# A new hand-written order, with limits on transfers in flight, for a chunked RWKV-7 attention and MLP kernel

## The chip, the cores and the metric

The kernel runs on one core of a Trainium2 chip. Its engines each run their own list of instructions: TensorE (PE, with its weight loads counted apart as PEld), VectorE (DVE), ScalarE (ACT), GpSimd (POOL) and SyncE (SP), which here does nothing but issue DMA transfers. The engines wait for one another by semaphores. The metric is device time in microseconds (us), the median over several executions.

## The reference

The inputs r, k, v, w, a and b have 4 batches, 8 heads, 768 tokens and 40 channels, all in float32. For each batch and head a 40x40 state is carried along the tokens; then x, of 3072 tokens by 320 channels, goes through a two-layer MLP with a quick GELU.

```python
for t in range(S):
    y[:, :, t] = einsum('bhd,bhde->bhe', r_t, state)
    Sa = einsum('bhde,bhe->bhd', state, a_t)
    state = state * w_t[:, :, None, :] - einsum('bhd,bhe->bhde', Sa, b_t) \
          + einsum('bhd,bhe->bhde', v_t, k_t)
x = y.transpose(0, 2, 1, 3).reshape(3072, 320)
h = x @ w_in                                 # 320 -> 2048
out = (h / (1 + exp(-1.702 * h))) @ w_out    # 2048 -> 320
```

## The kernel before, in words

The 768 tokens are cut into 12 chunks of 64, and the 4 batches into 2 pairs: 24 units of one chunk and one pair. Within a unit the recurrence is solved as a triangular system of 64x64 for each head, so that nearly all work is small matmuls, four of them side by side in quarters of the array. A unit i goes through five steps; the line numbers are those of the profile:

- `decay` (from line 552) sums the logarithms of w on PE (`ps_cum`, `ps_cumc`) and takes their exponentials on ACT (`FT`, `GT`, `wch`, `G`).
- `prep` (from 627) scales the loaded operands by them: `ak` by `FT` at line 633 and by `GT` at 638, `b` at 635, `kh` and `bh` at 641, on DVE or POOL. PE forms the scores: `score_A` into `ps_A`, `score_RV` into `ps_RV`, and in the next step `score_N` into `ps_N`.
- `inverse` (from 676) inverts the triangular matrix by five `level`s. Each has matmuls into `ps_level`, copies to `W` (765) and `E` (767), a transpose `ES` (716) and a spreading `EX` (721 on ACT, 723 on DVE or POOL). `off_one` and `off_two` (`Tc` copies at 811, `ps_Q`, `ps_T`) join the blocks into `T` (844).
- `solve` (from 850) turns the state (`ps_zT`), reads it (`ps_rz`, copied to `zr` at 883), builds `B` (905, 908), multiplies by `T` (`ps_X`, `M` at 921), and forms the output and the new state in one group `ps_y`. The output is copied (956) and scaled (966, `x`), written to DRAM (`part_with`) and read back turned (`get_back`, into `xT`).
- After the second unit of a chunk comes `mlp(c)` (from 991): eight groups q of `ps_up` matmuls, each followed by one GELU on ACT (1004) into one of four `g` tiles, then for each pair the `ps_down` matmuls, a copy and an add into the one `ob` tile (1031, 1033), and a store. In the last group the 320 columns are done in two halves.

Tiles have few slots: two each for `ak`, `b` and `rv`, three for `xT`, one for `x` and `ob`. The PSUM is used as four pairs of banks; which pair a result gets is part of the order.

All this is recorded as 2709 tasks. `Plan.listed` (line 89) then reads the string `ORDER` (line 109): one word for each task, with its number, a letter for its engine (p PE, d DVE, a ACT, g POOL, s SP) and a digit. The tasks are issued in exactly this order, so each engine runs its own in this order; an engine that waits holds back everything listed for it later. For p, d, a and g the digit is the PSUM pair. For s, the transfers, it is `t.window`, a limit which `transfer` (line 331) turns into a wait:

```python
begun.append(queue.dma_start(dst, src).ins)
if t.window and len(begun) > t.window:
    tc.add_manual_dep(begun[-1], begun[-1 - t.window].name, ...)  # few transfers under way
```

A word `330s4` means: task 330 is issued on SP, and it waits until the transfer that was begun four before it has landed. No digit means no limit. One task can begin two transfers. All transfers go through SP's queue, except one half of the last store, which ACT issues.

Of the kernel before, what the change touches and what calls it, by code (L numbers as in the profile page):

```python
# [124 lines left out]
56d 480s 479s3 78s4 481g 482d 57d 327d3 380d0 81s4 570a 236p1 59g 392a2 389p0 237p1 328d3 393d2 329g 330s4 390a0 484g 238p1  # L125
73a 486p3 487d3 240p0 491p3 74d 239a1 381p2 472s4 492d3 473s 493d3 241p0 494a3 382d2 242p0 485d 529d 394p2 79s 488p1 75d 76d
339a 489d1 530p3 532a3 496d 243p0 251p1 395d2 531a3 497a 82a 77g 340d 252p1 557s3 558s4 548p3 83d 85d 396p2 495d 549a 244p0
84d 245p0 550a3 338s4 397d2 86g 253p1 398d2 533p2 551g 399g 534a2 554a 254p1 498p2 500d2 560s4 501d 562d 568p3 499a2 331s 609d
246p0 247p0 556s4 559s4 535p2 255p1 561d 474a 248a0 569d3 249d0 400s 401s2 571p3 536d2 610p0 256p1 572d3 475d 564d 563d 257p1
612a0 574a3 258p1 573d3 576d 575d 577d 537p2 402p3 502g 403p3 404p3 611a0 250s 578p0 538a2 539d2 259a1 702s 566p2 405p3 580d0  # L130
581d 260d1 567d2 565g 406p3 407p3 579a0 503p1 408p3 504a1 582g 409p3 553s 505d1 410p3 694p2 424p1 425p1 426p1 613p0 427p1 703s
695a 706s 428p1 429p1 411p3 506d 696a2 583p2 555d 430p1 585d2 614d0 431p1 432p1 412a3 433p1 584a2 586d 446p3 507d 708d 508p0
699s 698s4 447p3 587d 552s 510d0 511d 434a1 413p2 512a 588p1 414p2 509d0 415p2 513p0 707d 590d1 591d 416p2 589a1 592d 417p2
785s3 593p1 700a 515d0 514d0 418p2 516d 709g 419p2 517d 420p2 421p2 518p0 595d1 594d1 519d0 523d0 422p2 782s2 524d0 520d 435p1
436p1 437p1 697d 438p1 423a2 521a0 525p2 704s2 439p1 526d2 440p1 522a0 441p1 716p0 596d 718d0 527p2 442p1 443p1 444p1 597g
528d2 445a1 719d0 540p2 448p3 598p1 717d0 720g 721d 261s2 722a 617p0 618a0 541d2 599d1 602d1 542p2 619d0 615p0 711g 601a1 600d
544d2 449p3 603a1 604a1 781s 723p1 616d0 605p0 450p3 606a0 607p0 451p3 452p3 710d 701d 545g 608d0 546s 783s 705s 927s 725d1
724d1 726d 543d2 620p0 727a 773p1 930s 778s 547s 453p3 621d0 774a 754d 728p2 622p0 454d3 455d3 729d2 456s 457p3 775a1 776g
730d2 784s 786g 779a 777s 624d0 458p3 623d0 625g 731d 793p1 833d 732a 459p3 733p2 789g 460p3 626s 734a2 794d1 735d2 714p0 790g
736d 461p3 780d 737g 1009s 918p1 755p2 923s 462p3 715d0 756a2 627s 757a2 788d 463p3 738p0 787d 464p3 739a0 740d0 919a 795p2  # L140
465d3 758p0 1006s 466d3 798a2 921d 650p3 467s 759d0 920a1 651p3 924a 928s 796d2 712p1 797d2 652p3 922s 800d 799g 653p3 932d
801a 654p3 834p0 655p3 713d1 656p3 657p3 835d0 760p2 836d0 925d 658p3 761a2 659p3 762p1 660a3 741d 628p0 742d 926s 629p0 630p0
763d1 802p2 764d1 631p0 803a2 804d2 632p0 805d 633p0 806a 743p3 634p0 746d3 635p0 747d3 837p1 931g 748d3 636p0 838a1 1007s
749d3 637p0 807p2 744d3 933g 638a0 639p1 808d2 640p1 791p3 745a 809d2 672p0 810d 792d3 811a 750p2 641p1 751a2 812p3 642p1
813a3 814d3 752p2 643p1 753d2 644p1 815d 645p1 816a 765p3 839p2 766d3 646p1 840a2 647p1 817p3 648p1 818a3 819d3 767p2 820d
649a1 821d 673p0 769d2 929s 768d2 770g 822p3 934d 674p0 825a3 826a3 940p1 827a3 675p0 1151s 828a3 935d 943a1 771s 661p2 823d3
662p2 941d1 1154s 824a 663p2 942d1 997p3 945d 944g 664p2 998a 1002s 978d 938p1 946g 665p2 939d1 666p2 772s 667p2 668p2 829p1
669p2 999a3 1000d 1001s 830d1 670p2 1003a 1011d 676p0 671a2 1004d 831p3 841p1 677p0 832d3 1005s 842d1 936p3 843d1 678p0 937d3
844p2 679p0 845d2 947p1 1010g 680d0 846p3 948a1 681d0 1012d 682s 683p2 847d3 1013g 1008s 848d3 1019p0 1014g 949d1 684p2 1022a0
1230s 849d 1233s 979p3 685p2 980a3 950d 850s 1020d0 981a3 951g 1142p1 1021d0 686p2 1024d 1143a 1147s 1023d 1025g 982p3 1057d  # L150
687p2 1152s 952p0 851s 983a3 1145g 688p2 1156d 1146s 953a0 954d0 984p3 1144a1 955d 1148a 689p2 956d 985a3 1149d 986p0 690p2
987a0 1150s 988d0 957p1 691a2 863p3 958a1 692d2 864p3 959d1 865p3 693s 960d 866p3 961d 1026p0 867p3 1027a0 1028d0 868p3 1029d
1155g 869p3 1157d 1030a 1058p2 870p3 871p3 1059a2 872p3 1060d2 1031p1 873a3 852p0 1033d1 853p0 1034d 854p0 1035d 1061p2 855p0
1062d2 1032a1 856p0 962p3 857p0 963a3 964d3 1036p1 965d 858p0 1037a1 1038d1 859p0 1039d 1015p2 966a 1040g 860p0 1016d2 861p0
967p3 862a0 874p1 968d3 875p1 970d3 969g 1041p2 971d3 876p1 1042a2 972d3 877p1 973d3 878p1 879p1 1043d2 1017p0 1044d 974p3
1045a 880p1 1018d0 1231s 881p1 975a3 1164p2 882p1 1167a2 1165d2 1375s 976p0 883p1 1166d2 896p3 1169d 1168g 884a1 977d0 885p2
1170a 1046p0 989p1 1049a0 886p2 1050a0 990d1 887p2 1051a0 888p2 1052a0 889p2 1047d0 991p1 1048a 1065p0 992d1 1158g 1153s 890p2
1159d 1066a0 891p2 892p2 1067d0 1378s 893p2 1202d 1063p0 993d1 894p2 994d 1064a0 1229s 1053p1 897p3 895a2 1054d1 995s 1171p0
1221p2 898p3 1172a0 1173d0 1226s 1174d 1222a 1175g 1055p1 899p3 1056d1 1068p0 996s 1162p1 1223a2 1224d 1234g 1225s 1069d0
900p3 1227a 1163d1 1160p2 901p3 1236d 1161d2 902p3 1235d 1176p0 1228d 903p3 1177a0 1178d0 1243p1 904a3 1179d 1070p2 1246a1  # L160
1454s 905d3 1180g 1244d1 906s 1245d1 907p0 1248d 1232s 1237g 1071d2 1249a 908p0 1238g 1072d2 1247d 1181p3 1457s 1281d 1366p1
909p0 1182a3 1073d 1371s 910p0 1183d3 1367a 1074s 1184d 1250p2 1185d 911p0 1368a1 1369g 1370s 1380d 1251a2 1186p3 1252d2 1372a
912p0 1253d 1188d3 1254g 1075s 1187a3 1189d 1241p1 1373d 913p0 1190g 1255p2 914p0 1242d1 1256a2 1257d2 1203p3 915d0 1204a3
1191p1 916d0 1205a3 1087p2 1258d 917s 1194a1 1088p2 1259d 1089p2 1195a1 1206p0 1196a1 1090p2 1197a1 1207d0 1376s 1091p2 1092p2
1192d1 1208p3 1193a 1093p2 1209d3 1210p0 1094p2 1211a0 1374s 1198p1 1095p2 1212d0 1199a1 1096p2 1239p3 1097a2 1076p0 1240d3
1077p0 1200p1 1078p0 1201d1 1079p0 1213p3 1379d 1381g 1080p0 1081p0 1214d3 1260p1 1082p0 1261a1 1262d1 1083p0 1263d 1215p2
1264a 1084p0 1217d2 1382g 1377s 1085p0 1386p3 1216d2 1086a0 1383g 1109p1 1426d 1110p1 1602s 1445p2 1111p1 1218d 1450s 1112p1
# [986 lines left out]
```

## Time and profile before

| what | us |
|---|---|
| median of 3 runs | 683.46 |
| lowest and highest run | 681.78, 684.25 |
| the profiled execution | 679.52 |
| its span, first to last instruction | 677.8 |
| PE busy | 651.0 |
| DVE busy | 456.7 |
| ACT busy | 325.2 |
| POOL busy | 174.8 |

The span is that of the one profiled execution; its time is longer by what lies before the first and after the last instruction. A row of a table of groups gives the line, engine, operation, the tiles written and read, their shapes, the count, then the busy time in us and the mean in ns of one instruction, and last the idle time of the engine before them with what ended it. In the chain of work a piece has its start, its length and what ran; "issue" is time in which the engine waited for nothing that the profile shows. In the timeline a row joins successive like instructions; the time in brackets is idle time before them. The profile's page gives PE's instructions twice the number of matmuls in the program, since an fp32 matmul is carried out in two passes.

### The profile page before, as it was taken

Reading aid. Unit: us, or ns where it says so; the run is one execution under the profiler, and the core shown is the slowest. Engines: PE = TensorE matmul, PEld = TensorE weight load, DVE = VectorE, ACT = ScalarE, POOL = GpSimd, SP = SyncE. Lnnn points to the kernel's source line nnn. Section 1 sums busy time; section 2 is a strip of 40 time slices with the busy share of each in tenths; the row PEclk is TensorE's granted clock in tenths of the full one; section 3 lists DMA queues with packets and bytes.
Section 4 is the critical chain, followed back from the end, with each engine's and each line's share of the span. In section 5 each row is a group of like instructions: output and inputs, shape, how many; then the busy total and the mean of one; then the engine's idle time right before and its main releaser. Section 6 shows DMA issues by size and latency. Waiting matters only on the chain.

```text
span 677.8 us, 42456 instructions
## 1 busy us (share of the span) xinstructions
PE 651.0 (96%) x19616; PEld 558.0 (82%) x19616; DVE 456.7 (67%) x923; ACT 325.2 (48%) x669; POOL 174.8 (26%) x212
## 2 busy tenths in 40 slices
PE   5687999999999999999999999999999999999997
PEld 5576878887999998888888898898889797788776
DVE  6679788777867758757776687868666766675001
ACT  4664564454564654574445455455354354263010
POOL 5235445115123223223213211222411321300000
PEclk9969999999999999999999999999999999999999
DMA  6855665416314414432404513513412411200200
GB/s 209 278 177 173 191 186 162 131 36 184 108 38 134 124 36 124 124 102 81 127 14 126 152 36 108 154 34 107 146 33 69 123 53 46 70 14 14 60 13 21
DMA packets 35473, 69.74 MB, mean 103 GB/s; under 512 B 5472, under 2 KB 14816, under 8 KB 35296
## 3 DMA queue, kind: packets, MB, share of 16 engines
q1 hardware_dynamic: 35216, 66.99, 32.9%
q8 instruction: 154, 2.52, 1.6%
q14 instruction: 23, 0.19, 0.1%
q10 hardware_dynamic: 80, 0.04, 0.0%
HBM read 59.15 MB, written 7.86 MB: 99 GB/s over the span
## 4 chain that ended last, share of the span: by engine, by line
PE 86%; issue 4%; DMA 4%; DVE 3%; POOL 1%; ACT 1%; SPq 0%; DVEq 0%; POOLq 0%; ACTq 0%
PE ps_down L303 29%; PE ps_up L303 28%; PE ps_level L303 8%; PE ps_y L303 5%; PE ps_B L303 4%; PE ps_X L303 2%; PE ps_N L303 2%; PE ps_A L303 1%; PE ps_RV L303 1%; PE ps_rz L303 1%; PE ps_zT L303 1%; PE ps_cum L303 1%; PE ps_T L303 1%; PE ps_Q L303 1%; DMA rv<-in_rv 1%
## 5 line engine op out<-in xcount | busy, mean ns | idle before, releaser
L303 PE MATMUL ps_up<-xT_all,w_sb 64*64 64x256 f32 x3840 | 250.5, 377 | 1.9 <-ACT PT L798 1.0
L303 PE MATMUL ps_down<-w_sb,g 64*64 64x320 f32 (+1 forms) x3200 | 239.7, 419 | 0.2 <-ACT zr L883 0.2
L303 PEld LDWEIGHTS ps_up<-xT_all,w_sb 64*64 64x64 f32 x3840 | 166.5, 133 | 20.4 <-issue 2.6
L303 PEld LDWEIGHTS ps_down<-w_sb,g 64*64 64x64 f32 x3200 | 134.6, 133 | 38.2 <-ACT zr L883 0.4
L1004 ACT ACTIVATE g<-ps_up 128x1024 f32<-128x1024 f32 x48 | 49.1, 1025 | 48.9 <-PE ps_up L303 48.6
L723 POOL TENSOR_TENSOR EX<-ES,quads 128x512 f32<-128x512 f32 x29 | 38.6, 1333 | 124.4 <-DVE ES L716 96.3
L765 ACT COPY W<-ps_level 128x512 f32<-128x512 f32 x55 | 32.2, 586 | 68.0 <-PE ps_level L303 64.3
L303 PEld LDWEIGHTS ps_level<-W,EX 64*64 64x64 f32 x2560 | 58.7, 134 | 6.2 <-ACT EX L721 0.6
L767 DVE TENSOR_TENSOR E<-two,ps_level 128x256 f32<-128x256 f32 x80 | 33.2, 416 | 37.2 <-ACT W L765 29.5
L303 PE MATMUL ps_level<-W,EX 64*64 64x64 f32 (+1 forms) x2560 | 55.7, 217 | 0.0
L721 ACT ACTIVATE EX<-ES,quads 128x256 f32<-128x256 f32 x78 | 35.4, 501 | 31.1 <-DVE ES L716 30.6
L633 POOL TENSOR_TENSOR ak<-ak,FT 128x512 f32<-128x512 f32 x17 | 21.8, 1284 | 81.8 <-DMA ak<-in_ak 59.9
L303 PEld LDWEIGHTS ps_level<-PT,EX 64*64 64x64 f32 x1280 | 30.6, 138 | 10.2 <-issue 4.4
L716 DVE STREAM_TRANSPOSE ES<-E 128x256 f32<-128x256 f32 x80 | 35.5, 444 | 4.7 <-DVE E L767 0.5
L303 PE MATMUL ps_level<-PT,EX 64*64 64x64 f32 (+2 forms) x1280 | 32.9, 234 | 5.8 <-issue 3.6
L303 PE MATMUL ps_y<-M,bh 64*64 64x104 f32 (+1 forms) x768 | 36.9, 253 | 1.0 <-issue 1.0
L303 PE MATMUL ps_y<-RV,kh 64*64 64x104 f32 (+1 forms) x768 | 36.8, 252 | 0.4 <-issue 0.4
L905 ACT COPY B<-ps_B 128x416 f32<-128x416 f32 (+1 forms) x33 | 16.2, 491 | 34.3 <-PE ps_B L303 34.1
L303 PEld LDWEIGHTS ps_y<-RV,kh 64*64 64x64 f32 x768 | 29.9, 137 | 2.5 <-issue 0.6
L303 PEld LDWEIGHTS ps_y<-M,bh 64*64 64x64 f32 x768 | 28.5, 137 | 1.6 <-issue 1.6
L921 DVE TENSOR_TENSOR M<-ps_X,later 128x832 f32<-128x832 f32 (+1 forms) x24 | 23.8, 993 | 8.8 <-PE ps_X L303 8.7
L303 PEld LDWEIGHTS ps_B<-RV,A 64*64 64x64 f32 x768 | 26.1, 141 | 4.1 <-DVE QT L832 0.7
(131 smaller groups left out, 1091.5 us busy)
## 6 DMA issues: line engine op xcount, KB each, us to landing
ak<-in_ak SPq DMA_DIRECT2D x48, 160.0 KB
rv<-in_rv SPq DMA_DIRECT2D x48, 160.0 KB
time<-in_time SPq DMA_DIRECT2D x24, 320.0 KB
xT_all<-x_dram SPq DMA_DIRECT2D x48, 160.0 KB
wc<-in_wc SPq DMA_DIRECT2D x20, 264.0 KB
logw<-in_w SPq DMA_DIRECT2D x24, 160.0 KB
RV<-in_v SPq DMA_DIRECT2D x24, 160.0 KB
b<-in_b SPq DMA_DIRECT2D x48, 80.0 KB
```

The source lines that it names most:

```text
L303: nc.tensor.matmul(o, lhsT, rhs, start=start, stop=True, skip_group_check=True)
L633: plan.add(R, {"DVE": 690.0, "POOL": 1270.0, "sbuf": True}, lambda t: of(t.engine).tensor_mul(ahT(), ahT(), FT_of(i)), reads=T("ak", "FT") ...
L716: plan.add(rank, dve(256), lambda t: nc.vector.transpose(ES(n), source(t)), writes=[key("ES", n, 6)], **reads)
L721: nc.scalar.activation(dst[:, :, h], ES(n), ACT.Copy, scale=quads[:, h, :1])
L723: of(t.engine).tensor_mul(dst, ES(n).unsqueeze(2).to_broadcast([128, 8, 2, 32]), quads.unsqueeze(1).to_broadcast([128, 8, 2, 32]))
L765: plan.add(rank, any2(512), lambda t: copy(t.engine)(tiles_of(W(n + 1)), blocks(psum(t, ""), 64)), writes=[key("W", n + 1, 5)], pair=pair)
L767: plan.add(rank, dve(256), lambda t: nc.vector.tensor_sub(tiles_of(E(n + 1)), every(two32, [128, 2, 4, 32]), blocks(psum(t, ""), 64)[:, :, ...
L905: plan.add(R, any2(4 * wide), lambda t: copy(t.engine)(dst(), some(psum(t, "")[:, :, :208])), writes=[("Bv", i)] if x and c > 0 else T("B" ...
L921: plan.add(R + 1, dve(8 * wide), lambda t: nc.vector.tensor_tensor(M_of(i)[:, :, :wide].rearrange("p (j b) n -> p b j n", b=2), some(psum( ...
L1004: plan.add(-45, {"ACT": 1030.0, "table": "gelu"}, lambda t: nc.scalar.activation(g_of(c * NQ + q).rearrange("p m r n -> p r m n"), psum(t, ...
```

## The change

Only the string `ORDER` changes. Its first 365 tasks stay as they are; the 2344 behind them stand in a new order. Some of them go to another engine or another PSUM pair, and the transfers get new limits.

```diff
-56d 480s 479s3 78s4 481g 482d 57d 327d3 380d0 81s4 570a 236p1 59g 392a2 389p0 237p1 328d3 393d2 329g 330s4 390a0 484g 238p1
-73a 486p3 487d3 240p0 491p3 74d 239a1 381p2 472s4 492d3 473s 493d3 241p0 494a3 382d2 242p0 485d 529d 394p2 79s 488p1 75d 76d
+56d 480s 479s3 78s4 481g 482d 57d 327d3 380d0 81s4 570a 236p1 59g 392a2 389p0 237p1 328d3 393d2 329g 390a0 238p1 73a 486p3
+487d3 240p0 381p3 529d 491p2 79s 485d 557s4 74d 382d3 494a2 241p0 82a 330s5 76d 75d 484d 493d2 556s 558s5 242p0 488p3 239a1
...
-2483s 2645p3 2646p3 2647p3 2648p3 2649p3 2650p3 2651p3 2652p3 2677p0 2653a3 2654p2 2655p2 2656p2 2657p2 2658p2 2659p2 2660p2
-2661p2 2662p2 2663p2 2678p0 2664a2 2665p1 2666p1 2667p1 2668p1 2669p1 2670p1 2671p1 2672p1 2673p1 2674p1 2679p0 2675a1 2680p0
-2681p0 2682p0 2683p0 2687p3 2684d0 2685d0 2688p3 2686s 2689p3 2690p3 2691p3 2692p3 2693p3 2694p3 2698p1 2695a3 2699p1 2696d3
-2700p1 2697s 2701p1 2702p1 2703p1 2704p1 2705p1 2706d1 2707d1 2708s
+2650p0 2471d1 2640p3 2641p3 2478p2 2654p1 2655p1 2656p1 2472s3 2651p0 2652p0 2657p1 2658p1 2659p1 2660p1 2661p1 2653a0 2662p1
+2642a3 2663p1 2479p2 2480p2 2665p3 2666p3 2664a1 2667p3 2668p3 2669p3 2670p3 2671p3 2672p3 2673p3 2674p3 2687p0 2688p0 2676p1
+2677p1 2689p0 2690p0 2481a2 2675a3 2482d2 2678p1 2679p1 2698p2 2680p1 2691p0 2681p1 2682p1 2692p0 2683p1 2699p2 2700p2 2693p0
+2694p0 2701p2 2702p2 2483s5 2684a1 2685d1 2686s3 2695a0 2703p2 2704p2 2696d0 2705p2 2697s4 2706a2 2707d2 2708s4
```

Task 556 is the load of `ak` of unit 5, 557 and 558 those of its `b` and `rv`; 2631 is the read back of the last chunk's x; 2686, 2697 and 2708 are the last three stores. Counted over the 2344 moved tasks:

| | before | after |
|---|---|---|
| SP tasks without a limit | 186 | 43 |
| limit 5 | 0 | 58 |
| limit 4 | 8 | 41 |
| limit 3 | 2 | 58 |
| limit 2 | 4 | 0 |
| tasks on DVE, in the whole order | 803 | 809 |
| on ACT | 418 | 402 |
| on POOL | 131 | 141 |
| on PE, on SP | 1088, 269 | 1088, 269 |

Of the moved tasks, the output's scaling (line 966) goes from DVE to POOL in 8 units and back in 2; the `Tc` copies (811) move from DVE to ACT 26 times and back 16 times; `W` copies (765), the spreads (721, 723) and the products with the loads (633 to 641) move in both directions.

More of the change, by code (lines that the diff above doesn't have):

```diff
@@ L128 @@
[L128 to L143, printed above, removed]
@@ new lines @@
+1215p3 1377s 1381d 1084p0 1109p1 1085p0 1110p1 1262d2 1380d 1086a0 1226s 1263d 1216d3 1282p2 1111p1 1382d 1112p1 1113p1 1383d
+1284a2 1217d3 1283a2 1218g 1386p3 1445p0 1219s5 1446a 1114p1 1264d 1285p2 1426d 1115p1 1116p1 1117p1 1370s5 1118p1 1286d2
+1447a0 1387d3 1265p0 1267d0 1120p3 1119a1 1450s 1266a0 1289p2 1098p1 1287p0 1099p1 1290a2 1100p1 1101p1 1102p1 1103p1 1268d
+1269d 1291d2 1388p2 1288d0 1104p1 1453s 1391d2 1390d2 1448g 1270p0 1274a0 1121p3 1105p1 1106p1 1389d2 1427p2 1458g 1393d
+1276a0 1271d0 1428a2 1107p1 1459d 1272d 1429a2 1394d 1122p3 1273d0 1275d0 1123p3 1430p2 1392g 1599s3 1108a1 1277p1 1467p0
@@ new lines @@
+1431a2 1469d0 1468d0 1124p3 1278a1 1279p1 1395p2 1451a 1125p3 1472d 1470d0 1280d1 1455s 1396d2 1126p3 1397d2 1457s 1292p1
+1471g 1384p0 1372a 1293d1 1460g 1473g 1127p3 1294p1 1385d0 1128a3 1602s5 1296d1 1295d1 1129d3 1297g 1398d 1456s4 1131p2 1220s4
+1399a 1298s3 1434p0 1474p1 1465p3 1476d1 1477d 1475d1 1466d3 1132p2 1133p2 1134p2 1400p1 1478d 1432p3 1435d0 1402d1 1461g
+1462d 1135p2 1436d0 1433a3 1373d 1136p2 1590p3 1401d1 1299s4 1137p2 1463p1 1300p0 1464d1 1598s3 1403d 1130s3 1301p0 1591a
+1592a3 1138p2 1479p3 1404d 1481d3 1405p1 1406a1 1604d 1482d 1302p0 1407d1 1139a2 1408d 1303p0 1304p0 1305p0 1311p1 1409d
@@ new lines @@
+1956d1 1957p1 1865a 1771p2 1936g 2045d 1937p0 1939d0 1772p2 1773p2 1958a1 1774p2 1938d0 1870p1 1775p2 2060p0 1776p2 1777p2
+1871a1 1872p1 1778p2 2062d0 2063d0 1873d1 1779p2 2061d0 1940d 1885p1 1886d1 1781p0 1780a2 1782p0 1783p0 1959p2 1941a 1942p1
+2053d 2048s3 1960d2 1943d1 1944g 1784p0 1785p0 1786p0 1887p2 1900d 1945a1 1888d2 1787p0 1788p0 2054g 1946a1 1947a1 1948a1
+1889d2 2065d 2064d 1789p0 2066g 1790p0 1949p1 1961p2 1793p3 1950a1 1951p1 1952d1 1962a2 1791a0 1794p3 2049s3 2055g 2058p0
+1963d2 1890g 2117p1 1589s5 2067p2 2118a 2069d2 1795p3 2125s3 1891s5 2098d 2274s 2059d0 2070d 2119a1 2068a2 2121s5 1796p3
@@ new lines @@
+2127s3 2120d 2099p1 2071g 1797p3 1964p0 2072p2 2101a1 1798p3 1799p3 2123a 2131d 1965d0 1800a3 2074d2 1966p0 2073a2 2130g
+2100d1 2132d 2134d 1801d3 1968d0 1967d0 2139p1 1803p2 1804p2 1969g 2102p3 2140d1 2142a1 1892s 2141d1 2056p0 2103a3 1970s5
+2122s5 2133d 1805p2 2057d0 2262p3 2144d 2143d 1806p2 2128s5 2106p0 2137p1 2138d1 1807p2 1808p2 2107d0 1971s 2075d 2145a 1802s5
+2263a 2104p1 2264a3 2351s3 2177d 2108d0 1809p2 2146p3 1810p2 2268a 2105a1 2148d3 2178p1 2124d 2135p0 2179d1 2147a3 2270s5
+2149d 2180a1 2076d 1972p3 1811a2 1973p3 1974p3 2150a 1812d2 1975p3 1976p3 1977p3 2136d0 1978p3 1979p3 2151p1 1980p3 2153d1
@@ new lines @@
+2009p3 2287d2 2097d0 2164d 2165a 2010p3 2109p0 2265d 2286d2 1813s4 2011p3 2285d2 2110d0 2166p2 2172a2 2018p1 2288d 2167d2
+2183p0 2012p3 2171a2 2170a2 2013p3 2289d 2184d0 2169a2 2014p3 2185p2 2347s 2168d 2266s4 2186d2 2111p0 2278g 2015a3 2173p3
+2187d2 2174a3 2112d0 2019p1 2113d0 2175p3 2176d3 2020p1 2279g 2188p2 2114g 2322d 2189d2 2341p3 2323p0 2021p1 2022p1 2342a
+2324d0 2115s5 2190p2 2343a3 2489s4 2290d 2352d 2345a 2023p1 2325d0 2280p3 2191d2 2192d2 2353d 2024a1 2027p0 2291p2 2281d3
+2273s4 2355d 2028p0 2293d2 2350s3 2025d1 2361p3 2326p1 2363d3 2193g 2292d2 2116s5 2327a1 2026s4 2354g 2194s5 2356d 2362d3
```

194 lines of the change are left out of this document (93 added, 101 removed).

## The prediction

> **What bounds the kernel now.** I read the page's span, busy shares and chain by engine first, then the table of stretches, then what TensorE (PE) waits for behind the opening, then the trains of matmuls in the timeline.
>
> ```profile
> span 677.8 us, 42456 instructions
> PE 651.0 (96%) x19616; PEld 558.0 (82%) x19616; DVE 456.7 (67%) x923; ACT 325.2 (48%) x669; POOL 174.8 (26%) x212
> PE 86%; issue 4%; DMA 4%; DVE 3%; POOL 1%; ACT 1%; SPq 0%; DVEq 0%; POOLq 0%; ACTq 0%
> 100.00:150.00 50.00, 49.73 (x1410) 42.62 (x1401) 38.96 (x75) 26.11 (x50) 16.08 (x15) 1.00 0.39 117
> 150.00:200.00 50.00, 48.73 (x1538) 43.27 (x1532) 37.06 (x73) 24.96 (x55) 13.93 (x19) 1.00 0.38 109
> 200.00:250.00 50.00, 50.00 (x1554) 48.09 (x1550) 35.04 (x74) 30.44 (x64) 14.78 (x15) 1.00 0.34 101
> 500.00:550.00 50.00, 49.56 (x1517) 42.38 (x1513) 32.73 (x66) 23.71 (x56) 13.74 (x16) 1.00 0.26 76
> 640.00:677.80 37.80, 33.92 (x685) 27.47 (x676) 2.44 (x6) 4.82 (x6) 0.00 (x0) 1.00 0.06 15
> ```
>
> TensorE is the bound: 86% of the chain. The stretch rows give length, then busy time of PE, PEld, DVE, ACT and POOL, clock, DMA share and GB/s. From 100 us on PE is idle for 0.27, 1.27 and 0.44 us in three stretches and 0 in the others before the last; the last 3.88 us are the tail. DVE, the next engine, stands at 39 of 50 us at most. The opening, where the large idle time lies, is outside the change, which begins at task 365 of the order (PE about 94 us).
>
> A busy PE can still be short of its best, so I put the columns of every matmul against the closest spacing that a train shows.
>
> ```profile
> 667.74 6.18 PE L303 MATMUL ps_down<-w_sb,g 64*64 64x160 f32 x176
> L303 PE MATMUL ps_up<-xT_all,w_sb 64*64 64x256 f32 x3840 | 250.5, 377 | 1.9 <-ACT PT L798 1.0 <-issue 0.7 <-PE ps_rz L303 0.2
> L303 PE MATMUL ps_X<-B,T 64*64 64x64 f32 x64 | 1.3, 218 | 0.0
> ```
>
> The train gives (6.18 - 0.30) / 175 = 33.6 ns for 160 columns, about 4.8 columns a ns. Over the 28 matmul groups of all 19,616 (first and last shown) the columns come to 606.8 us. The starts of successive matmuls exceed that by 12.6 us from 100 us to the tail. Of it 6.1 us lie in fifteen gaps of over 0.2 us behind 94 us; the other 6.5 us are spread over short matmuls. So 12.6 us is the ceiling of what any order can win here, and 6.1 us is what can be named.
>
> The named gaps are of two kinds:
>
> ```profile
> 97.97 3.85 DMA wc<-in_wc
> 101.84 3.62 DMA b<-in_b
> 105.93 4.01 DMA time<-in_time
> 110.00 3.21 DMA ak<-in_ak
> 113.68 1.07 DVE ak L633
> 114.39 0.87 PE L303 MATMUL ps_down<-w_sb,g 64*64 64x320 f32 x8
> 115.40 0.40 PE L303 MATMUL ps_N<-b,ak 40*64 40x64 f32 x12
> PE ps_y L303 <- issue: 1.0, 3, 0.4
> 150.60 0.25 PE L303 MATMUL ps_y<-M,bh 64*64 64x104 f32 x1
> 151.24 0.32 PE L303 MATMUL ps_y<-M,bh 64*64 64x104 f32 x4 [0.39 <-issue]
> q8 instruction: 154, 2.52, 1.6%
> ```
>
> The first kind is a late operand: the chain ran through four loads one behind another on SP's queue, each 3.2 to 4.0 us, then the ak product, and the score matmul began at 115.40, 0.41 us after the downs could hand over (114.39 + 8 x 0.067 = 114.93, and 0.06 of the last down). The second is PE waiting for nothing but its own instructions: a gap inside ps_y, with no semaphore. The instruction queue moved 2.52 MB in 154 packets, 16 KB or 256 instructions each, hence one per 128 matmuls or 4.4 us on average; its 1.6% of 16 engines' span is 1.13 us a packet. A block of short matmuls can be used up sooner than the next arrives.
>
> The Trainium skill, "Runtime: NRT & Kernel Launch", section "Instruction fetch mechanics", says that the fetch is hidden because instructions are dispatched more slowly than blocks arrive. This trace differs: the three ps_y gaps above are 1.0 us. By the page the second rival below could not occur; the sum stays as it is.
>
> **The change part by part.** The same tasks and matmuls remain; 2344 of them change place, some copies and products change engine, and the transfers behind the opening are limited: 58 of the 200 SP tasks wait for the fifth transfer before, 41 for the fourth, 58 for the third, where 186 had no limit.
>
> 1. The ak load of unit 5 (task 556) now stands 22 places behind the point where the orders part instead of 75, ahead of the wc load (task 472) that began at 97.97. It is issued near 98 us instead of 110.00, so the gap at 115 goes: -0.4 us. What is late next there is the time load, still behind ak on SP's queue, which the score does not read. Bounds: -0.4 to 0.
>
> 2. The other named gaps, 6.1 - 0.4 = 5.7 us. Late operands (zr, Q, up, score_RV) make some 2.9, gaps inside ps_y some 2.8. The new order meets the dependences anew. I counted PE's work between each result and its use in both orders against the row durations: short of zero by 0.9 us before (4 places) and 0.8 us after (8 places); under 0.6 us of spare in 65 places before and 57 after. Nothing there says that they vanish; the places differ, each costs 0.2 to 0.5 us. I take half: -2.8 us (bounds -5.7, all gone, and +2.8, half as many again).
>
> 3. Moved engine work. By these rows:
>
> ```profile
> L966 POOL TENSOR_TENSOR x<-zr,FT 128x128 f32<-128x128 f32 x44 | 22.9, 553 | 22.1 <-issue 11.7 <-DVE zr L956 10.4
> L966 DVE TENSOR_TENSOR x<-zr,FT 128x128 f32<-128x128 f32 x44 | 10.6, 299 | 0.4 <-DMA x_dram<-x 0.2
> L723 POOL TENSOR_TENSOR EX<-ES,quads 128x512 f32<-128x512 f32 x29 | 38.6, 1333 | 124.4 <-DVE ES L716 96.3
> L811 DVE COPY Tc<-ps_level 32x64 f32<-32x64 f32 x108 | 23.2, 215 | 2.5 <-ACT Tc L811 0.9 <-PE ps_level L303 0.2
> L811 ACT COPY Tc<-ps_level 32x64 f32<-32x64 f32 x84 | 17.0, 203 | 17.0 <-PE ps_level L303 9.5 <-DVE ES L716 4.7 <-DVE Tc L811 1.4
> ```
>
> In total ACT loses about 15 us, POOL gains about 19, DVE stays. All three stay below PE (POOL 194 of 678), so this counts only where a chain has little cover. The output scaling L966 goes to POOL in 17 of 24 units instead of 11: 4 x (553 - 299) = 1.0 us longer each. Its cover is the path of x through DRAM:
>
> ```profile
> 628.50 0.96 SPq L333 DMA_DIRECT2D x_dram<-x  x2
> 631.75 1.13 SPq L333 DMA_DIRECT2D out<-ob  x2
> 632.98 1.19 SPq L333 DMA_DIRECT2D xT_all<-x_dram  x2
> 636.99 1.28 PE L303 MATMUL ps_up<-xT_all,w_sb 64*64 64x256 f32 x20
> ```
>
> From the write at 628.50 to the first up that uses it are 8.5 us, 1.24 of them lost when SP stood at the store until 631.75. PE's work between the last y and that up falls from 10.8 to 9.7 us in the last chunk; the read back no longer stands behind that store. 1.1 us less cover against 1.2 us won: 0 (bounds -0.1 and +1.2). In the other chunks the cover is 11 to 16 us against 8 to 10 needed: 0. Moved copies: 0, hidden behind PE; if the cover is gone, 0.1 to 1 us a place, which is in the bounds of step 2.
>
> 4. The spread 6.5 us. 28 fewer changes of matmul form, and longer runs of one form; the trace shows some 0.02 to 0.04 us per change by starts: -0.8 us (bounds -2 and 0).
>
> 5. The limit on transfers. Each wait stands in SP's queue, with all later loads and stores behind it; the waits of SP show that it has idle time to give:
>
> ```profile
> SPq L333 <- DVE ob L1033: 80.1, 19, 20.1
> SPq L333 <- PE ps_y L303: 71.0, 11, 17.9
> SPq L333 <- DMA x_dram<-x: 23.1, 18, 3.1
> ```
>
> So SP mostly waits for buffers, not for transfers, and a wait for an earlier transfer mostly ends before: 0 for the likeliest. Bounds: -2 us (if fewer transfers at a time shorten the instruction packets, the ps_y gaps go) and +10 us (third rival).
>
> 6. Tail. The downs of the last two groups interleave now, and both last stores follow closely on one ob slot.
>
> ```profile
> 669.75 0.29 ACT L1031 COPY ob<-ps_down 128x160 f32<-128x160 f32 x1 [8.78 <-PE ps_down L303]
> 670.43 4.72 SPq L333 DMA_DIRECT2D out<-ob  x3
> 673.97 0.33 DVE L1031 COPY ob<-ps_down 128x160 f32<-128x160 f32 x1 [3.57 <-PE ps_down L303]
> 674.68 0.56 ACTq L333 DMA_DIRECT2D out<-ob  x1
> ```
>
> Before, the store at 670.43 had 4 us before the last. Now the group before the last ends about 1 us before it, and its stores take SP's time (0.55 each) in front of the last one. The end itself, copy 0.33, add 0.32, store 3.1, stays: +0.4 us (bounds 0 and +1).
>
> Sum: -0.4 - 2.8 + 0 - 0.8 + 0 + 0.4 = -3.6 us. The profiled execution took 679.52 us, 677.8 of span and 1.7 around it, and would go to 675.9. It stands 3.9 us below the median of the runs, 683.46. PE's work is the same in both, so I take those 3.9 us for further gaps of the kinds of step 2 and halve them as well: -2.0 us. On the median: 683.5 - 3.6 - 2.0 = 677.9.
>
> **The rivals.**
>
> *The gaps only change place* (same). For it: step 2's counts, hardly different, and 50.00 busy of 50 in most stretches. Against it: the largest chain, at 97 to 113 us, is certainly cut. Only steps 1, 4 and 6 remain, -0.8 us: 682.7.
>
> *The instruction fetch falls behind* (slower). Taking columns alone, 0.5% of the blocks of 128 matmuls lasted under 3 us before and 2.3% after, the shortest 2.58 and 2.36 us; of 154 blocks that is 1 and 3 to 4. With 0.45 us a gap this is +1.2 us; it decides from some 16 further gaps (+7 us against the sum's 3.6), which would need blocks of 3 to 3.5 us to stall as well: 687.
>
> *SP's queue becomes the bound* (slower). Here the limit itself is the mechanism:
>
> ```profile
> 384.03 0.66 SPq L333 DMA_DIRECT2D ak<-in_ak  x2
> 387.99 1.28 POOL L633 TENSOR_TENSOR ak<-ak,FT 128x512 f32<-128x512 f32 x1 [9.33 <-DMA ak<-in_ak]
> ```
>
> Two transfers of 160 KB needed 3.9 us. Three at a time carry at most 3 x 160 KB / 3.9 us = 126 GB/s, three of 80 KB half of that, and five of 160 KB 210; the stretches from 100 to 250 us move 101 to 117. Where threes stand in a row in these stretches, SP falls behind, and the loads come late as at 97 to 113 us. Against it: the mean limit is four, later stretches need 76 and less. It decides once a held load passes its spare of 1 to 3 us in about ten places; with 0.4 to 1.1 us a place as at 115 us that is +4 to +11, so 690. The Trainium skill, "DMA: Bandwidth & Descriptors", section "Rules for kernel authors", advises to issue a DMA early and to wait for it late, which a limit works against; the trace agrees at 110.00, where a load issued late delayed PE. By that rule the time is the 690 of this rival.
>
> **How the numbers follow.** Fewer gaps 0.40 (677.9, own range 673.5 to 681); gaps only change place 0.24 (682.7); the fetch 0.10 (687); SP's queue 0.26 (690). A measurement tells about 0.5%, 3.4 us, from no change, so 680.0 and 686.9 are the limits. Of the first case 0.34 is faster and 0.06 the same; of the second 0.04 faster, 0.16 the same, 0.04 slower; of the fetch 0.05 each, same and slower; of SP's queue 0.24 slower, 0.02 the same. That makes faster 0.38, same 0.29, slower 0.33. The range leaves out a tenth at either side: below 674.0 only all named gaps gone, above 692.0 only a queue that is behind in most stretches.
>
> **What the profile will show.** Right: ps_N of unit 5 without the wait for ak around 115 us; idle PE from 100 to 640 us under 2 us; excess over columns below 10 us; the ps_y gaps as before or fewer; end of the last matmul to the end of the span 3.9 to 4.5 us. Wrong if PE waits for DVE or POOL products of ak and b, or for xT_all, at several places from 100 to 300 us, with SP's waits on its own transfers grown from some tens to over 100 us; or if the issue gaps inside ps_y, ps_B and ps_level go from three to over ten.

## The result and the profile after

The new kernel is slower: 685.51 us (681.63 to 687.35, 12 runs) against 682.06 us (679.88 to 686.02, 12 runs), a ratio of 1.0045 with a 95% interval of 1.0026 to 1.0064, so 1.8 to 4.4 us. That is below the half per cent that the prediction took as what a measurement tells, but the interval leaves out 1, and it has the other sign than the forecast. The page of the profiled execution after, its busy row and its chain by engine:

```profile
span 681.1 us, 42403 instructions
PE 651.8 (96%) x19616; PEld 583.7 (86%) x19616; DVE 446.2 (66%) x901; ACT 309.6 (45%) x650; POOL 189.6 (28%) x240
PE 88%; DMA 5%; DVE 4%; issue 1%; ACT 1%; SPq 1%; ACTq 0%; DVEq 0%
```

The span grew by 3.3 us, as the timed runs did. ACT lost 16 us and POOL gained 15, DVE lost 10. The table of stretches of the new kernel (length, busy time of PE, PEld, DVE, ACT and POOL, clock, DMA share, GB/s):

```profile
100.00:150.00 50.00, 49.86 (x1454) 44.23 (x1450) 39.05 (x76) 22.51 (x46) 18.25 (x15) 1.00 0.37 109
150.00:200.00 50.00, 49.71 (x1588) 44.97 (x1579) 37.20 (x78) 26.81 (x53) 15.35 (x21) 1.00 0.33 93
400.00:450.00 50.00, 48.99 (x1506) 43.08 (x1501) 32.51 (x72) 24.64 (x52) 18.17 (x21) 1.00 0.37 105
640.00:681.10 41.10, 36.56 (x729) 35.12 (x721) 1.61 (x4) 5.42 (x8) 0.00 (x0) 0.99 0.06 14
```

The idle time at 150 to 200 us shrank from 1.27 to 0.29 us, as hoped, but 1.01 us stand at 400 to 450 now, where none was, and the tail grew. Over all from 100 to 640 us PE's idle time hardly differs, 1.98 us before and 2.10 after. To see where time is won and lost I put the two traces side by side by the columns of matmuls done (of 606.8 us at 4.8 columns a ns). At the end of the common part both stand at 94.6 us. The new kernel is 1.9 us ahead at 240 us of columns (290 us of the span), level at 360, 2.3 us behind at 460, 0.8 behind at 500, 2.5 behind at 540 (607 us), and the tail adds 0.6. So it is a handful of gaps, and not a stage.

What the waits of PE behind 94 us name, in the new kernel, and the largest gap in its timeline:

```profile
PE ps_down L304 <- issue: 0.8, 3, 0.3
PE ps_RV L304 <- issue: 0.7, 1, 0.7
PE ps_level L304 <- issue: 0.3, 1, 0.3
PE ps_T L304 <- ACT QT L831: 0.3, 1, 0.3
PE ps_level L304 <- DVE zr L957: 0.2, 1, 0.2
444.79 0.56 PE L304 MATMUL ps_RV<-rv 40*64 40x64 f32 x15
446.04 0.50 PE L304 MATMUL ps_RV<-rv 40*64 40x64 f32 x17 [0.69 <-issue]
```

The late operand of unit 5 is gone, and so are the three gaps in ps_y. In their place PE stops in the middle of ps_RV, ps_level and ps_down groups, again with no semaphore. I sorted all gaps behind 94 us (eight successive starts over 0.25 us later than their columns allow) by their place in PE's stream, counting its weight loads, matmuls and semaphore instructions from the first, modulo 256:

```
before   gap us at  count%256      after   gap us at  count%256
         0.43  101.38  190                 0.83   98.53  193
         0.35  124.71  193                 0.37  103.45  192
         0.66  151.24  193                 0.26  293.32  192
         0.37  164.31  192                 0.56  437.70  192
         0.32  169.12  192                 0.97  446.04  193
         0.70  197.10  192                 0.61  474.34  192
         0.48  527.49  193                 0.79  594.73  193
 other   2.5 in 5 gaps                     3.5 in 9 gaps
```

The gaps listed by time stand inside groups of like matmuls, and all at the same place of a block of 256 instructions; the others stand mostly where PE goes from one group to the next and waits for a result. One of 0.25 us in the middle of a ps_down group (589.75 us, count 176) has no known cause. In each of the listed gaps the last packet of the instruction queue had ended 1.1 to 1.7 us before PE went on. So these are waits for instructions, here called boundary gaps. They sum to 3.3 us before and 4.4 us after, the others to 2.5 and 3.5 us. With the tail (0.6) and the remaining small differences (0.5) this makes the 3.3 us of the two spans. Each trace is one execution.

### The profile page after: what moved, and what is told of

It reads as the page before. It is cut to its first block, busy times and chain, and to the rows that moved or that the text cites. A ratio compares the mean times of both kernels' runs of the same rounds, so it can differ in the third digit from the quotient of the medians.

```text
span 681.1 us, 42403 instructions
## 1 busy us (share of the span) xinstructions
PE 651.8 (96%) x19616; PEld 583.7 (86%) x19616; DVE 446.2 (66%) x901; ACT 309.6 (45%) x650; POOL 189.6 (28%) x240
## 4 chain that ended last, share of the span: by engine, by line
PE 88%; DMA 5%; DVE 4%; issue 1%; ACT 1%; SPq 1%; ACTq 0%; DVEq 0%
PE ps_up L304 30%; PE ps_down L304 30%; PE ps_level L304 8%; PE ps_y L304 4%; PE ps_B L304 4%; PE ps_X L304 2%; PE ps_N L304 2%; DMA b<-in_b 2%; DMA extra<-in_w_in 2%; PE ps_RV L304 1%; PE ps_A L304 1%; PE ps_rz L304 1%; PE ps_zT L304 1%; PE ps_T L304 1%; DMA w_sb<-in_w_in 1%
## 5 line engine op out<-in xcount | busy, mean ns | idle before, releaser
L304 PE MATMUL ps_up<-xT_all,w_sb 64*64 64x256 f32 x3840 | 247.9, 377 | 1.4 <-ACT PT L799 1.0
L304 PEld LDWEIGHTS ps_up<-xT_all,w_sb 64*64 64x64 f32 x3840 | 178.9, 134 | 11.6 <-issue 2.8
L304 PEld LDWEIGHTS ps_down<-w_sb,g 64*64 64x64 f32 x3200 | 150.8, 133 | 31.4 <-issue 2.8
L766 ACT COPY W<-ps_level 128x512 f32<-128x512 f32 x50 | 29.2, 584 | 58.7 <-DVE E L768 46.4
L1034 DVE TENSOR_TENSOR ob<-ob,ps_down 128x320 f32<-128x320 f32 (+1 forms) x25 | 11.7, 467 | 49.3 <-ACT ob L1032 49.0
L967 POOL TENSOR_TENSOR x<-zr,FT 128x128 f32<-128x128 f32 x68 | 32.6, 510 | 39.0 <-issue 23.5
L812 ACT COPY Tc<-ps_level 32x64 f32<-32x64 f32 x104 | 21.0, 202 | 38.6 <-DVE ES L717 17.3
L634 POOL TENSOR_TENSOR ak<-ak,FT 128x512 f32<-128x512 f32 x18 | 23.5, 1303 | 49.9 <-DMA ak<-in_ak 25.4
L722 ACT ACTIVATE EX<-ES,quads 128x256 f32<-128x256 f32 x60 | 27.1, 501 | 21.0 <-DVE ES L717 20.8
L1032 ACT COPY ob<-ps_down 128x320 f32<-128x320 f32 (+1 forms) x19 | 7.8, 412 | 57.5 <-PE ps_down L304 53.4
```

The lines of the kernel that those rows point to most:

```text
L304: nc.tensor.matmul(o, lhsT, rhs, start=start, stop=True, skip_group_check=True)
L634: plan.add(R, {"DVE": 690.0, "POOL": 1270.0, "sbuf": True}, lambda t: of(t.engine).tensor_mul(ahT(), ahT(), FT_of(i)), reads=T("ak", "FT") ...
L722: nc.scalar.activation(dst[:, :, h], ES(n), ACT.Copy, scale=quads[:, h, :1])
L766: plan.add(rank, any2(512), lambda t: copy(t.engine)(tiles_of(W(n + 1)), blocks(psum(t, ""), 64)), writes=[key("W", n + 1, 5)], pair=pair)
L812: copy(t.engine)(dst, src[:, u, :, f])
L967: of(t.engine).tensor_mul(x[:, b ^ u, b], y, FT_of(i)[:, at])
```

## The experiments

All ratios are to the kernel before, run beside it on the same chip. There were three theories: the limits on transfers cost the time (theory 1), the places of the tasks do (theory 2), or the instruction fetch does (theory 3).

**Limits away, and limits alone.** In the new order:

```diff
-... 557s4 ... 330s5 ... 558s5 ... 560s5 ... 473s3 ... 703s4 ...
+... 557s ... 330s ... 558s ... 560s ... 473s ... 703s ...
```

> The new order with every limit on transfers behind the opening taken away (the digits of the SP tasks from task 365 on), nothing else changed. Theory 1, the limits hold loads back and that is the loss: the time falls by 2 to 4 us, to the level of the kernel before or under it. Theory 2, the places of the tasks make the loss: no change beyond 1 us. Theory 3, instruction fetch is what suffers and more transfers at a time make it wait longer: up to 2 us slower, with more gaps inside matmul groups at the places where a block of 256 instructions begins.

Measured: 687.95 us (686.39 to 690.34, 6 runs), ratio 1.0106 (1.0074 to 1.0139): slower than the new kernel with its limits (1.0045) by 0.6%. Theory 1 falls for the new order; the limits help it. The gaps at block boundaries sum to 9.1 us instead of 4.4, the others to 3.8 (3.5). The largest, in the timeline of this run and the DMA share of the 40 slices of 0.2 us from 131 to 139 us:

```profile
135.80 0.64 PE L303 MATMUL ps_level<-W,EX 64*64 64x64 f32 x28
138.34 0.27 PE L303 MATMUL ps_level<-W,EX 64*64 64x64 f32 x2 [1.90 <-issue]
DMA  7659997999989979988656682010100000000000
q8 instruction: 1, 0.02, 0.8%
```

PE crossed into the block before this gap at 131.84 us. The one packet of the instruction queue in the window began only at 135.74, when the DMA engines came free (the digits fall from 9 to 2), and ended at 136.78; PE went on at 138.34. Over all blocks behind 94 us the packet begins 0.6 us behind the crossing in the kernel before and 0.85 us in the new one (medians). So this packet most likely stood behind loads. Theory 3 has the sign right, but not the size: up to 2 us were expected, and 0.6% is about 4 us. Theory 2 (no change) falls as well.

The other way round, the new limits on the order before:

```diff
-... 557s3 558s4 ... 560s4 ... 556s4 559s4 ...
+... 557s4 558s5 ... 560s5 ... 556s 559s4 ...
```

> The order before with the new order's limits on each transfer (task by task), nothing else changed. Theory 1 (the limits hold loads back): 2 to 4 us slower than the kernel before. Theory 2 (the places of the tasks): within 1 us of it. Theory 3 (fetch): the same or up to 1 us faster, with shorter waits of the instruction packets.

Measured: 688.48 us (684.48 to 690.91, 6 runs), ratio 1.0103 (1.0068 to 1.0138). In this order the limits cost 7 us, more than the 2 to 4 of theory 1; theory 2 (within 1 us) and theory 3 (the same or faster) fall. The waits of PE behind 94 us and a piece of the chain of this run:

```profile
PE ps_up L305 <- DMA xT_all<-x_dram: 3.4, 2, 2.0
PE ps_y L305 <- issue: 1.2, 3, 0.7
174.30 3.64 DMA xT_all<-x_dram
178.08 0.63 PE ps_up L305
```

The read back of x stands behind limited loads on SP's queue, and PE waits for it twice, 2.8 and 2.4 us by the starts. In front of the second, SP stood 1.8 us until the load of time and 0.5 us until that of b had landed. The boundary gaps did not shrink in this order: 4.4 us against 3.3. In the new kernel no wait for xT_all stands in the list. The limits and the order belong together: in the old order they hold the read back, in the new one they don't.

**Joined orders.** Each task list can be continued by the other where every open PSUM pair and dependence allows it.

```diff
 new order, first 1061 tasks, then the order before:
 1157g 693s5 1048g
-994g 1158g 1067d0 1063p1 895a2 ...
+1147s 1375s 1158g 1159d 1067d0 1378s ...
 order before, first 1061 tasks, then the new order:
 1159d 1066a0 891p2 892p2
-1067d0 1378s 893p2 1202d ...
+893p2 993d1 894p2 994g 1067d0 ...
```

> The first 1061 tasks in the new order with its limits (to about 254 us), the rest in the order before; at this point the two orders differ in only four tasks. Measured by the columns of matmuls done, the new kernel's trace is 1.7 us ahead at 250 us and 4.3 us behind that lead at the end. If the places of the tasks decide: about 1.7 us faster than the kernel before, so near 680.4 where that has 682.1. If the limits decide, or if a gain early is given back later whatever stands there: no faster than the kernel before.

Measured: 681.82 us (677.74 to 684.81, 12 runs), ratio 1.0007 (0.9984 to 1.0029). No gain.

> The first 1061 tasks in the order before, the rest in the new order with its limits: the opposite of the last one. If the places of the tasks decide: 4 to 5 us slower than the kernel before (687), that is 1.7 us slower than the new kernel too. If the loss comes of something spread over the whole: between the two kernels.

Measured: 686.15 us (684.98 to 687.65, 6 runs), ratio 1.0077 (1.0049 to 1.0106): slower than the kernel before, as expected, and not less than the new kernel. Taking the four ratios together, the new order's part behind 254 us costs 0.38% with the new head and 0.77% with the old, its head -0.32% to +0.07%. The loss lies behind 254 us; the head's part is not clear of the noise. The two parts need not add up: 0.07% and 0.77% against 0.45% is within the sum of the intervals. A joint may make gaps of its own (the two traces have 6.2 and 6.0 us at block boundaries, where the kernels have 3.3 and 4.4), but that isn't shown.

**The end.** The new order to task 2479 (594 us), then as before, which undoes the interleaved last groups too:

```diff
 2510a3 2257p0 2582g
-2258p0 2513d 2418p1 2514p2 2259d0 2260d0 2516d2 2583p3 ...
+2571d 2513a 2258p0 2514p3 2259a0 2583p2 2515a3 2260d0 ...
```

> The new order up to task 2479 (about 594 us), the rest, with the tail, as before: at this point the orders differ in one task. If the tail is worth what the two traces show (last matmul to end of the span 4.5 against 3.9 us) and the gap at 595 us goes with it (0.8 us): 1 to 1.5 us faster than the new kernel, about 684.2. If neither counts: as the new kernel.

Measured: 682.53 us (680.15 to 684.1, 12 runs), ratio 1.0015 (0.9997 to 1.0033), against 1.0045: 2.0 us less, and the interval of that difference holds the 1 to 1.5 us expected. In the traces of the two kernels the new one lost 1.3 us around 595 us, behind 520 us of columns, and 0.6 in the tail. In the trace of this run, the slowest of its 12 executions (684.1), the tail is back at 3.9 us, but a gap at 596.7 us is larger (1.4 us). So of the 2.0 us the trace shows only the 0.6 of the tail; where the rest was won isn't shown. The tail of the new kernel, from its timeline:

```profile
672.68 6.07 SPq L334 DMA_DIRECT2D out<-ob  x5
675.99 0.29 ACT L1032 COPY ob<-ps_down 128x160 f32<-128x160 f32 x1 [3.86 <-DMA out<-ob]
676.60 0.29 ACT L1032 COPY ob<-ps_down 128x160 f32<-128x160 f32 x1 [0.32 <-PE ps_down L304]
676.92 0.32 DVE L1034 TENSOR_TENSOR ob<-ob,ps_down 128x160 f32<-128x160 f32 x1 [0.29 <-ACT ob L1032]
677.27 0.56 ACTq L334 DMA_DIRECT2D out<-ob  x1
```

The copy at 675.99 waited for an earlier store to land, since there is one ob tile, and five stores follow closely on SP's queue. SP issues its half of the last store only at 677.95, 0.7 us behind the add, since two halves of earlier stores go first. From the last matmul to the end are 4.5 us instead of 3.9.

**Fewer bytes.** From unit 6 on, rv, RV and time keep their old data except for a slice (the tiles of RV and time are the old ones, taken again). What the kernel leaves out is the rest of these loads, so its output is another one:

```diff
+if i >= 6 and name in ("rv", "RV", "time"):
+    dst, part = dst[:, :40] if len(dst.shape) == 2 else dst[:, :1], ...
 transfer(t, dst, part)
```

> The new order; from unit 6 on the loads of rv, RV and time bring an eighth or less of their bytes into tiles that keep the old data (the rest of these operands is left out, so the output is another one). All tasks, waits, limits and transfers stay. If PE's gaps at the block boundaries come from instruction packets that stand behind loads on the DMA engines: from 110 us on these gaps fall from some 3.2 us to under 1 us, and the time by 3 to 5 us against the new kernel. If the gaps have another cause: they stay, and the time falls by under 1.5 us.

> The order before with the same loads cut down from unit 6 on. If transfers are the cause of the gaps: the boundary gaps behind 110 us fall from 2.9 to under 1 us, and the time by 2 to 4 us against the kernel before. What is left between this and the last run is then what the places of the tasks cost without any crowding: about 1.6 us by the gaps at handovers and the tail. If crowding is not the cause, the two differ by the same 3.4 us as the kernels themselves.

Measured: 680.85 us, ratio 1.0001 (0.9977 to 1.0025), and 679.41 us, ratio 0.9968 (0.9941 to 0.9995), 10 runs each. One row each for 94 to 640 us, of the new kernel, of the cut new one and of the cut old one:

```profile
94.00:640.00 546.00, 543.56 (x16506) 484.27 (x16502) 372.23 (x772) 253.22 (x523) 150.75 (x177) 1.00 0.31 91
```

```profile
94.00:640.00 546.00, 544.56 (x16514) 477.61 (x16509) 372.21 (x772) 252.77 (x523) 150.18 (x177) 1.00 0.26 75
```

```profile
94.00:640.00 546.00, 543.15 (x16593) 475.64 (x16588) 382.70 (x798) 270.66 (x548) 138.43 (x150) 1.00 0.26 76
```

The cut was smaller than I meant: 91 to 75 GB/s. The new kernel gains 3.0 us and the old one 2.2, as expected. The boundary gaps behind 110 us fall from 3.2 to 1.8 us in the new order, not to under 1, and in the old one they don't fall at all (2.9 and 3.3; its trace is the slowest of its 10 executions, 682.93). So crowding is not their only cause, and what the old order gained isn't found in its trace. Two gaps of the kernel before, at 151 and 197 us, stand where no transfer runs. Around the first, the DMA share from 147 to 152 us in slices of 0.125 us, and the packets of that window:

```profile
DMA  0000000000000004000000000000000000000000
GB/s 0 0 0 0 0 0 0 0 0 0 0 0 0 0 0 131 0 0 0 0 0 0 0 0 0 0 0 0 0 0 0 0 0 0 0 0 0 0 0 0
q8 instruction: 1, 0.02, 1.1%
```

The only thing on the DMA engines is the instruction packet itself (148.94 to 149.86), and PE waits until 151.24. The block before it lasted 3.2 us from its crossing (147.41) to the stop (150.6); from the crossing to the restart are 3.8 us, of them 1.5 to the begin of the packet, 0.9 for the packet and 1.4 behind it. A short block alone does not stall: in the same trace the one that begins at 238.92 lasts 3.2 us and has no gap behind it, since its packet began 0.3 us after the crossing. And a packet can be late on idle engines. This is the run `a_shift`, described below, from 569 to 576 us; PE crossed at 569.64, the only packet began at 572.28, and a gap of 1.0 us ends at 574.90, behind a block of 4.2 us:

```profile
DMA  0000000000000000004000000000000000000000
q8 instruction: 1, 0.02, 1.2%
574.90 1.24 PE L304 MATMUL ps_up<-xT_all,w_sb 64*64 64x256 f32 x17 [0.69 <-issue]
```

Busy engines do go with later packets: where the engines were under a tenth busy around the crossing (1.2 us), the median is 0.5 us before and 0.7 after; where they were over six tenths busy, 0.9 and 1.2. What else delays a packet stays open. The two cut kernels differ by 0.33%, the uncut by 0.45%; the intervals overlap, so how much of the difference is crowding stays open.

**Moving the block boundaries.** Small matmuls are added in the opening, into columns that nothing reads, and nothing else changes:

```diff
+for n in range(32 if i == 0 else 0):     # 16 in the quarter shift
+    e, b = n % 2, n // 2 % 2
+    mm(ps[HALF[e], b, 300:301], logw_t[0][HALF[b], :64], edges[HALF[b], :1], False)
```

> The order before, with 32 matmuls of one column added to the first unit's cumc task in the opening, where PE waits anyway: 128 instructions, half a block. If the gaps inside groups of like matmuls belong to blocks of 256 instructions: none stays where it was (ps_y at 151 and 197 us, ps_up at 125), new ones stand at the same residue of the count, 192 to 193, that is half a block away, with a sum of 1 to 5 us; the time moves by under 2 us either way. If they belong to the matmuls (ps_y, which reads and writes most): they stay in ps_y at 151 and 197.

Measured: 685.62 us (683.06 to 689.31, 8 runs), ratio 1.0067 (1.0039 to 1.0096). In the trace the gaps in ps_y at 151 and 197 us and in ps_up at 125 are gone; seven new ones stand at residue 192 to 193 (the remainder of the count by 256), 3.3 us in all, as much as before. The gaps at handovers stay at the same matmuls (ps_N 0.8, Q 0.5, up 0.5 us). The time is 4.5 us up, more than expected. The two traces differ by 4.1 us, 2.8 of them before 82 us and 1.3 behind. The 2.8 us arise between 73 and 82 us, long behind the added matmuls (5.2 to 6.8 us), and a boundary gap of 2.1 us stands there at matmuls where the kernel before has none:

```profile
73.16 0.37 PE L303 MATMUL ps_level<-PT,EX 64*64 64x96 f32 x7
75.30 0.54 PE L303 MATMUL ps_level<-PT,EX 64*64 64x96 f32 x14 [1.77 <-issue]
```

> The new order with the 32 added one-column matmuls of the shifted run before, which move the block boundaries by half a block. If block boundaries set the gaps inside groups: none left at 293, 438, 446, 474 and 595 us at the matmuls where they were, others elsewhere at residue 192 to 193, summing to 2 to 6 us. If the time that the other shifted run lost (5 us) came of the added matmuls in the opening: this one loses some 3 us against the new kernel too, all before 80 us; if it came of where boundaries fall, this one stays within 2 us of the new kernel, either way.

Measured: 690.61 us (689.46 to 695.95, 6 runs), ratio 1.0145 (1.0108 to 1.0181). None of the five gaps is left at its matmuls. Twelve boundary gaps behind 94 us sum to 9.6 us instead of 4.4, more than the 2 to 6 expected. Another 2.4 us are lost before 82 us, again at a boundary gap of 2.1 us (76.2 us). So it came of where boundaries fall, but the run did not stay within 2 us of the new kernel.

> The new order with 16 added one-column matmuls instead of 32: the block boundaries move by a quarter of a block. If it is chance where boundaries fall: the sum of the gaps at boundaries is another one again (between 2 and 10 us), and the time follows it, 684 to 692. If the loss of the shifted run (7 us) came of the added matmuls themselves: about half of it, with the gaps at boundaries as large as in the new kernel (4.4 us).

Measured: 695.19 us (693.04 to 698.26, 6 runs), ratio 1.0206 (1.0176 to 1.0235). Half as many added matmuls cost more, so it isn't the matmuls. From 35 to 40 us of columns the three shifted traces take 8.9, 7.5 and 6.7 us, the other traces 5.1 to 5.2. Each shifted one has a boundary gap of 1.6 to 2.1 us there, at 75 to 76 us; so the loss in the opening lies at boundaries too. Behind 94 us nineteen boundary gaps sum to 14.7 us; the other gaps stand at 3.4 us, as in the new kernel (3.5). PE's waits behind 94 us in this run:

```profile
PE ps_level L304 <- issue: 2.8, 3, 2.1
PE ps_N L304 <- issue: 2.0, 3, 1.5
PE ps_down L304 <- issue: 1.1, 1, 1.1
PE ps_up L304 <- issue: 1.0, 3, 0.6
```

Same order, same transfers, same engines: where the 256-instruction boundaries fall was worth 10 us of these gaps here, and 1.6% of the time (1.0206 against 1.0045).

**Engines.** The new places with every task on its old engine (299 tasks go back):

```diff
-... 484d ... 399d ... 561g ... 563g ... 536a2 ... 611d2 ...
+... 484g ... 399g ... 561d ... 563d ... 536d2 ... 611a2 ...
```

> The new order in places, PSUM pairs and limits, but every task on the engine that it has in the order before (299 tasks go back: Tc and W copies, spreads, the scaling of x, products). If the moved engine work costs nothing, as forecast, and the new places were not found for just these engines: within 1.5 us of the new kernel. If the longer steps on POOL (510 to 553 ns instead of 299 for the scaling) or ACT's late QT (gap of 0.7 us before ps_T at 155 us) are the loss: 1 to 3 us faster. If places and engines only work together: 2 to 6 us slower, with gaps of PE at handovers well over the 3.5 us of the new kernel.

Measured: 709.7 us (707.02 to 712.19, 6 runs), ratio 1.0412 (1.0376 to 1.0447), far beyond the 2 to 6 us expected. The gaps at handovers sum to 28 us in 40 places; PE's first waits behind 94 us:

```profile
PE ps_Q L304 <- DVE Tc L812: 2.7, 2, 2.0
PE ps_RV L304 <- DVE W L766: 1.1, 1, 1.1
PE ps_rz L304 <- ACT zT L873: 0.9, 1, 0.9
```

The new places can't be costed without their engines. The old places with the new engines were not run.

**A version that beats both?** The stretches in which each order came out ahead, joined:

```diff
 new order, its first 1061 tasks
+order before, what is left of its first 2186 tasks
+new order, what is left of its first 2368 tasks
+order before, what is left
```

> The stretches in which each order came out ahead, joined where they differ by few tasks: new to task 1061, before to 2186, new to 2368, before to the end. By the columns done in the two traces: -1.7, then +0, -1.5, 0, so 3 us faster than the kernel before. By the joined run that was already measured (new to 1061, then before: no faster) the first gain is not kept: then 1 us or less. If block boundaries and transfers make the gaps anew wherever neighbours change, no faster at all.

Measured: 681.6 us (678.89 to 686.63, 12 runs), ratio 0.9995 (0.9966 to 1.0024). Its trace is 3.1 us ahead at 360 us of columns (1.6 of it before 80 us, in the unchanged opening), and gives most of it back in gaps around 564, 591 and 600 us. It is faster than the new kernel (1.0045), but not than the one before.

## Why the prediction was wrong

- **Direction.** Forecast 677.9 us, measured 685.51; the range of 674 to 692 holds it, but the forecast was a gain of 5.6 us and the measured change is a loss of 3.4. The nearest of the four cases by its time was the fetch (687), to which I gave 0.10, then the gaps that only change place (682.7); what the traces show fits neither alone.
- **Step 1, the ak load: right.** No gap at ps_N of unit 5 is left. But at 97 to 103 us the new order has 0.83, 0.25 and 0.37 us of gaps where the old one had 0.43, so the 0.4 us is given back there.
- **Step 2, the named gaps: this is the step that failed.** I halved them for no reason that a row gave: my own count of spare said that the new order has nearly as many tight places (57 against 65) and eight short ones against four. In place of the -2.8 us the list of gaps over 0.25 us grew by 2.1, from 5.8 to 7.9 us. Over half of it were waits for instructions, and for these the count of spare says nothing at all: they hang on where a boundary falls, which I didn't look at. The sorting into two kinds was wrong too: the gap in ps_RV at 164.31, which I had put under late operands (score_RV), stands at a boundary, as do those in ps_down, ps_up and ps_zT. Waits for instructions were 3.3 of the 5.8 us, and the three in ps_y are 1.8 of them, where I had some 2.8.
- **The step to the median: wrong.** I took 3.9 us between the profiled run and the median for more gaps and halved them too. In the traces without added matmuls the unchanged opening alone ends (40 us of columns) anywhere from 77.1 to 82.4 us. A difference of that size between two executions is no store of gaps to be won.
- **Step 3, moved engine work at nothing: not as put.** PE's gaps outside the boundaries grew by 1.0 us, among them ps_T behind ACT's QT (0.7 us by the starts at 155 us). DVE lost 10 us, where I had it unchanged. In the new places the old engines cost 25 us more, so no term of this step stands by itself. The cover of x held: no wait for xT_all.
- **Step 4, the spread part: wrong.** Forecast -0.8 us; what is left outside of the gaps and the tail rose by some 0.5 us (3.3 of the spans, less 2.1 of gaps and 0.6 of tail). The 12.6 us that this step starts from do not follow from the columns either: at 4.8 columns a ns the starts from 100 us to the last matmul exceed the columns by 26.3 us before and 28.1 after, some 10 us of it before in the ps_level groups alone. So neither the ceiling nor the 6.5 us spread over short matmuls holds by this count.
- **Step 5, the limits at nothing: wrong, in both directions.** In the new order they are worth 0.6% (9.1 us of boundary gaps without them, 4.4 with); in the old one they cost 1.0%, and 5.2 us of the gaps in its trace stand where the read back of x came late.
- **Step 6, the tail: right**, 0.6 us against 0.4 forecast, by the mechanism given.
- **The rivals.** The fetch was priced at +1.2 us and came to +1.1. The mechanism is right, the number luck: I counted blocks under 3 us, one before and three to four after, but there are seven boundary gaps in each trace, behind blocks that lasted 3 to 4.6 us. It is a third of the loss, beside the other gaps (1.0), the tail (0.6) and the rest (0.5); I had asked it to overcome a gain that wasn't there. A late transfer on SP's queue as the bound happened only with the old order.

What stays open: each trace is one execution, so which of the gaps stand in every run isn't shown, and so the split of the 3.4 us by kinds is read from two traces and not shown by the timed runs. These show that the part behind 254 us carries the loss, and that some 2 us of it go with the order behind 594 us.

## What to carry to other kernels

When the bounding engine is busy for all but 2% behind the opening and a change only reorders, list its gaps one by one and give each a cause before forecasting that any goes away; with no cause removed, "the gaps change place" is the forecast. Look at gaps without a semaphore by their place in the engine's instruction stream: here they came with short blocks of instructions and late packets, and a few inserted matmuls moved them all. An order, its engines and its limits on transfers belong together here: the limits alone, and the new order with its engines but without limits, each cost 7 us against the kernel before, and the new places and limits without their engines 28 us.

## What the runs showed of the hardware that I had not expected

- PE's instructions came in blocks of 256, one packet a block (154 packets for some 39,500 instructions), and not far ahead: the packet began 0.6 to 1.0 us (medians of the runs) after a boundary was crossed, took 0.9 to 2.0 us, and where PE had stopped it went on 1.1 to 1.9 us after the packet's end. Packets were never closer than 3.2 us. Blocks that lasted 2.5 to 4.8 us from the crossing to the stop were followed by a gap with idle DMA engines too, but not every block of 3.2 us was.
- With the DMA engines full a packet began up to 3.9 us after the crossing (`a_free`, 135.74 us). On idle engines 2.6 us were seen as well (`a_shift`, 572.28 us), so loads are not the only thing that delays it.
- A shift of all boundaries by 64 or 128 instructions changed the sum of these waits from 4.4 to 14.7 and 9.6 us. In the first of these runs the gap at one boundary reached 2.4 us.
